# Pooling k of three batches on GpSimd and a DMA transpose in place of TensorE, in a pooled attention followed by a mixer

## The chip, the cores and the metric

The kernel runs on one core of a Trainium2 chip. The metric is device time in microseconds (us) of one execution. Three runs of the kernel before gave 282.7, 284.07 and 284.22 us, a median of 284.07. The profile comes from one further execution of 283.01 us, whose span (first to last recorded instruction) is 281.1 us. All places in time below are us from the start of that span.

## The reference

Inputs are `q`, `k`, `v` of shape (8 batches, 8 heads, 576 tokens, 64), and four weights. Everything is kept in float32 outside and bf16 inside the kernel.

```
k_p = k.reshape(B, H, 72, 8, 64).mean(axis=3)        # pool 8 neighbouring tokens
v_p = v.reshape(B, H, 72, 8, 64).mean(axis=3)
scores = scale * q @ k_p^T ;  attn = softmax(scores)  # 576 x 72 per head
x = (attn @ v_p) as (batch, 576 tokens, 512 channels)
u = x + (relu(x^T @ w_tok1) @ w_tok2)^T               # token mixing
out = u + relu(u @ w_ch1) @ w_ch2                     # channel mixing, 512 -> 1536 -> 512
```

So each batch needs its keys pooled from 576 to 72 tokens and laid out with the 64 head channels on partitions, before its first score can be computed.

## The kernel before

**Tiling.** The 576 tokens of a batch are 512 "main" tokens (4 tiles of 128) and 64 "tail" tokens. Tails of two batches share one 128-row tile: the groups are (0, 7), (1, 2), (3, 4), (5, 6). For the groups (3, 4) and (5, 6) one `TailUnit` computes the tail scores of both batches in one go, so `TailUnit.do_S` (L423, matmuls L431) of batches 5 and 6 needs the pooled keys of 5 **and** of 6.

**Pooling k (`pool_k`, L259 to L285).** k is loaded with 4 tokens on a partition (`km`, 128 partitions) and a tail tile `kt`. 32 matmuls (L271) with `km` as the stationary operand against a 0/1-over-8 matrix `pool_m`, and 8 more (L275) for the tail, leave the pooled and transposed keys in two PSUM banks. Four copies (L284, L285; two on ScalarE, two on VectorE) put them into `kbd`, a block form in which one matmul scores two heads. There are three `kbd` buffers.

**Pooling v (`sum_v`, L296).** For batches above 1, v is loaded with all 8 tokens of a pool on one of 72 partitions (`vs`, two buffers, L133), and GpSimd adds them up in 12 instructions (L302, L303, L304, four of each) into `vpx`.

**Order of the work.** Instructions are issued in an order written out by hand: every engine, and the SP queue that issues output writes and DMA transposes, executes its own instructions strictly in that order. The backbone is `c_stream(b)`, the channel mixing of batch b: 12 pieces `do_GT` (4 matmuls each, L776; called GT below) and 12 pieces of output (4 matmuls each, L791; three pieces make one 128-token block, after which VectorE adds u at L801 and SP writes it out at L829; called o0.0 to o3.2), plus a tail block for every second batch. `weave` (L29) mixes into it a side stream that prepares later batches:

- `value_stream(b+1)` (L731): on SP, the DMA transpose of q of b+2 (`qT_dma`, L550); on GpSimd, `load_gated` (L750) of b+3, which copies one element of a finished probability transpose (L752), then issues the loads, then runs `sum_v`; on TensorE the value products `do_AV`; then the token mixing (`mix_stream`, L580: `do_AT`, `do_u`, and a DMA transpose `do_uT` on SP), with `pool_k` of b+2 after the two `do_AT` (where b+2 opens a group or stands alone in one).
- `score_stream(b+2)` (L701): for the two units a and c of the batch, `do_S` for three banks of heads (matmuls L330, then VectorE max L333 and subtract L335), `do_E` (exponential on ScalarE, L343), `do_PT` (DMA transpose of the probabilities on SP, L350); `pool_k` of the group's second batch between the scores of c; last the tail's `do_S`, `do_E`, `do_PT`.

`weave` goes by written costs (KP 900 for a `pool_k`, SC 1060 for a bank of scores, AV 1150, 690 for a `do_u`, 1080 for a `do_AT`, 864 for a piece of the main stream): the side stream starts once `delay` cost units of the main stream are done and is spread evenly so that it ends `lead` units before the main stream does, 1728 units or two pieces here.

PSUM has six rotating 2 KB banks named `pa`, used by nearly all products. The part of the program that matters most below is `c_stream(3)`, which carries `value_stream(4)` and `score_stream(5)`; it runs from 128.45 to 158.00 us.

Of the kernel before, what the change touches and what calls it, by code (L numbers as in the profile page):

```python
# [10 lines left out]
AF = mybir.ActivationFunctionType  # L11
ALU = mybir.AluOpType
# [3 lines left out]
class Stream:  # L16
# [5 lines left out]
    def add(self, cost, fn):  # L22
        self.items.append((cost, fn))
# [25 lines left out]
def kernel(  # L49
# [17 lines left out]
    nc = tc.nc  # L67
    B, H, S, D = q.shape
    P = 128
# [3 lines left out]
    POOL = 8  # L73
    SP = S // POOL
# [31 lines left out]
    group_of = {b: g for g, members in enumerate(groups) for b in members}  # L106
    slot_of = {b: members.index(b) for members in groups for b in members}
    half = [slice(0, TAIL), slice(TAIL, P)]
    main_t, tail_t = {}, {}
    x_main, x_tail, u_main, uT_main, u_tail, uT_tail, ATs = {}, {}, {}, {}, {}, {}, {}  # L110

# [7 lines left out]
    def load(b, which=(0, 1, 2)):  # L119
        g = group_of[b]  # L120
        if b not in tail_t:
            tail_t[b] = [tail_pool.tile([P, H, D], BF16, name=n) for n in ("kt", "qt")]
            if b == 2:
                for t in tail_t[b]:
                    nc.gpsimd.memset(t[half[0]], 0.0)
            else:
                tail_t[groups[g][1]] = tail_t[b]
        main_t.setdefault(b, [None] * 3)
        for i in which:
            src = (k, q, v)[i]  # L130
            if i == 2 and b > 1:

                vs = v_pool.tile([P, H, POOL, D], BF16, name="vs")  # L133
                for r in (slice(0, SPM), slice(SPM, SP)):
                    nc.gpsimd.dma_start(out=vs[r].rearrange("p h t d -> p h (t d)"),
                                        in_=src[b].rearrange("h (p t) d -> p h (t d)", t=POOL)[r])
                main_t[b][i] = vs
                continue
            mt = (v_pool.tile([P, H, POOL, D], BF16, name="vs")[:, :, 0:NJ, :] if i == 2 else
                  kv_pool.tile([P, H, NJ, D], BF16, name=("km", "qm")[i]))  # L140
            main_t[b][i], tt = mt, tail_t[b][i]
            nc.gpsimd.dma_start(out=mt.rearrange("p h j d -> p h (j d)"),
                                in_=src[b, :, 0:MAIN, :].rearrange("h (p j) d -> p h (j d)", j=NJ))

            for bb in [b] if g < 2 else groups[g] if slot_of[b] == 0 else []:
                nc.gpsimd.dma_start(out=tt[half[slot_of[bb]]], in_=src[bb, :, MAIN:S, :].rearrange("h p d -> p h d"))
# [49 lines left out]
    NB = 3  # L196
    kbd = [singles.tile([P, H, 2, SP], BF16, name=f"kbd{i}") for i in range(NB)]
    vpx = [singles.tile([SP, H, D + 1], BF16, name=f"vpx{i}") for i in range(NB)]
    for i in range(NB):
        eng = nc.vector if i == 0 else nc.any  # L200
        eng.memset(kbd[i], 0.0)
        eng.memset(vpx[i][:, :, D], float(POOL))

    NPB = 4
    prob_m = [singles.tile([P, 2, H, P], BF16, name=f"prob_m{i}") for i in range(NPB)]
    prob_t = [singles.tile([P, 2, HP, P], BF16, name=f"prob_t{i}") for i in range(2)]
# [52 lines left out]
    def pool_k(b):  # L259
        pool_k_copy(b, pool_k_sum(b))  # L260

    def pool_k_sum(b):
        g, s = group_of[b], slot_of[b]
        km, kt = main_t[b][0], tail_t[b][0]
        kp_ps = [ps.tile([P, HP, SP], FP32, name="pa") for _ in range(2)]
        if b == 0:
            keep_running(kp_ps[0].rearrange("p r n -> p (r n)"), 22)
        for pr in range(HP):
            for j in range(NJ):
                for hl in range(2):  # L270
                    nc.tensor.matmul(out=kp_ps[hl][hl * D:(hl + 1) * D, pr, 0:SPM], lhsT=km[:, 2 * pr + hl, j, :],  # L271
                                     rhs=pool_m[:, 0:SPM], start=(j == 0), stop=(j == NJ - 1))
        for pr in range(HP):
            for hl in range(2):
                nc.tensor.matmul(out=kp_ps[hl][hl * D:(hl + 1) * D, pr, SPM:SP], lhsT=kt[:, 2 * pr + hl, :],  # L275
                                 rhs=pool_t[s][:, SPM:SP], start=True, stop=True)
        return kp_ps
# [17 lines left out]

    def sum_v(b):  # L296

        vs, add = main_t[b][2][0:SP], ALU.add
        for h0 in range(0, H, 2):
            hs = slice(h0, h0 + 2)  # L300
            s4 = sum_pool.tile([P, 2, 4, D], FP32, name="s4")[0:SP]
            nc.gpsimd.tensor_tensor(out=s4, in0=vs[:, hs, 0:4], in1=vs[:, hs, 4:8], op=add)  # L302
            nc.gpsimd.tensor_tensor(out=s4[:, :, 0:2], in0=s4[:, :, 0:2], in1=s4[:, :, 2:4], op=add)  # L303
            nc.gpsimd.tensor_tensor(out=vpx[b % NB][:, hs, 0:D], in0=s4[:, :, 0], in1=s4[:, :, 1], op=add)  # L304

    class Unit:

# [31 lines left out]
        def do_E(self, i):  # L339
            h0, h1 = BANKS[i]  # L340
            if self.probs is None:
                self.probs = prob_m[(2 * self.b + self.jj) % NPB]
            nc.scalar.activation(out=self.probs[:, :, h0:h1, 0:SP].rearrange("p e h n -> p h e n"),  # L343
                                 in_=self.sh[i][:, 0:(h1 - h0) * 2].rearrange("p (h e) n -> p h e n", e=2),
                                 func=AF.Exp, scale=scale)

        def do_PT(self, e):
            self.pT[e] = pt_pool.tile([P, H, P], BF16, name="pT")
# [54 lines left out]
    class TailUnit:  # L403
# [39 lines left out]
        def do_E(self):  # L443
            self.probs = prob_t[self.g % 2]
            for i, sh in enumerate(self.sh):
                nc.scalar.activation(out=self.probs[:, i, :, 0:SP], in_=sh[:, 0:HP], func=AF.Exp, scale=scale)

        def do_PT(self):
            n = len(self.bs) * HP
# [130 lines left out]
    def mix_stream(st, b, pooled=()):  # L580

        g, s = group_of[b], slot_of[b]
        add = adder(st)
        if b:
            u_main[b] = u_pool.tile([P, NJ, DM], BF16, name="um")
        uT_main[b] = u_pool.tile([P, 4, MAIN], BF16, name="uTm")
        if s == 1:
            u_tail[g] = ut_pool.tile([P, DM], BF16, name="ut")
            uT_tail[g] = ut_pool.tile([P, 4, P], BF16, name="uTt")
        do_AT, do_both_AT, do_u, do_uT, do_xT, do_uT0 = token_mix(b)  # L590
        if b == 0:
            return do_both_AT, do_xT, do_uT0
        add(1080, do_AT, 0)
        add(1080, do_AT, 1)
        for bb in pooled:
            add(KP, pool_k, bb)
        nj = NJ + s
        for j in range(nj + 1):
            if j < nj:
                add(690, do_u, j)  # L600
            if j >= 1:
                add(0, do_uT, j - 1)
# [93 lines left out]
    def owned(b):  # L696

        g, s = group_of[b], slot_of[b]
        return [b] if g < 2 else groups[g] if s == 0 else []

    def score_stream(st, b):  # L701

        add = adder(st)
        a, c, t = parts[b]
        own = owned(b)
        if b == 3:
            add(KP, pool_k, b)
        add(SC, a.do_S, 0)
        add(SC, a.do_S, 1)
        add(0, a.do_E, 0)  # L710
        add(SC, a.do_S, 2)
        add(0, a.do_E, 1)
        add(0, a.do_E, 2)
        add(0, a.do_PT, 0)
        add(0, a.do_PT, 1)
        add(SC, c.do_S, 0)
        for bb in own[1:]:
            add(KP, pool_k, bb)
        add(SC, c.do_S, 1)
        add(0, c.do_E, 0)  # L720
        add(SC, c.do_S, 2)
        add(0, c.do_E, 1)
        add(0, c.do_E, 2)
        add(0, c.do_PT, 0)
        add(0, c.do_PT, 1)
        if t:
            add(2 * SC, t.do_S)
            add(0, t.do_E)
            add(0, t.do_PT)

    def value_stream(st, b):  # L731

        add = adder(st)
        a, c, t = parts[b]
        if b + 1 < B:
            units(b + 1)
            add(0, qT_dma, b + 1)
        if b + 2 < B:
            add(0, load_gated, b + 2, lambda: t.pT[:, 0, 0:1] if t else c.pT[1][:, 0, 0:1])
        add(AV, a.do_AV, 0)  # L740
        add(AV, a.do_AV, 1)
        add(AV, c.do_AV, 0)
        add(AV, c.do_AV, 1)
        if t:
            add(AV, t.do_AV)
        mix_stream(st, b, owned(b + 1)[:1] if b + 1 < B and b != 2 else ())
# [3 lines left out]
    def load_gated(b, ready):  # L750

        nc.gpsimd.tensor_copy(out=gate, in_=ready())  # L752
        if b == 4:

            load(b - 1, (2,))
            load(b, (0, 2, 1))
            sum_v(b - 1)
        else:
            load(b, (0, 2, 1) if slot_of[b] else (0, 1, 2))
        sum_v(b)  # L760

    def channel_mix(uTs, us, dst, width, early=0):
# [91 lines left out]
    with tc.manual_schedule(engines=engines):  # L854
        weave(Stream(), first_stream())
        for b in range(B):
            side = Stream()
            if b == 0:
                second_stream(side)
            elif b + 1 < B:  # L860
                value_stream(side, b + 1)
            if b + 2 < B:
                score_stream(side, b + 2)

            weave(c_stream(b), side, (2592.0, 3456.0)[b] if b <= 1 else 1728.0, 3456.0 if b == B - 2 else 1728.0)


# [28 lines left out]
```

## Time and profile before

| what | value |
|---|---|
| median of three runs | 284.07 us (282.7 to 284.22) |
| profiled execution | 283.01 us, span 281.1 us |
| TensorE busy | 270.1 us, 96% of the span |
| VectorE, ScalarE, GpSimd busy | 57%, 44%, 37% |
| GpSimd's last sum | 184.63 to 185.1 us; nothing after |
| `c_stream(3)`, start to end | 128.45 to 158.00 us |
| one `sum_v` on GpSimd | 12 instructions, 10.17 us (145.32 to 155.49) |

How to read it: the page gives busy time by engine, the span in 40 slices, the chain of work that ended last, and groups of instructions by line. The timeline lists instructions as start, duration, engine, line, operation and tiles, with the idle time just before and who ended it. A matmul's duration includes its way through the array; matmuls in sequence start closer together than they last. "SPq" rows are instructions of the SP queue, whose duration is the time that issuing took; a transfer lands later.

### The profile page before, as it was taken

The numbers are of one execution on the slowest core, as the hardware profiler recorded it, in microseconds if no ns is written. First come the engines' busy times: TensorE is split into PE (matmuls) and PEld (weight loads), VectorE is DVE, ScalarE is ACT, GpSimd is POOL, SyncE is SP. The second block draws the span as 40 slices with busy tenths as digits, with TensorE's granted clock in tenths as the row PEclk, the third lists the DMA queues.
The fourth block names the chain that finished last, engine by engine and source line by source line (L and its number), as shares of the span: only waits on it lengthen the run. The fifth ranks groups of instructions, "written<-read, shape, count | busy, mean of one in ns | idle before, by whom it ended". The sixth has DMA issues, their size and how long they took to land.

```text
span 281.1 us, 5671 instructions
## 1 busy us (share of the span) xinstructions
PE 270.1 (96%) x2221; PEld 146.2 (52%) x2258; DVE 161.1 (57%) x368; ACT 122.6 (44%) x223; POOL 104.4 (37%) x153
## 2 busy tenths in 40 slices
PE   6799999999999999999999999999999999999995
PEld 4575565565445444475545454475444444554463
DVE  4695297597559952784469753775369542520012
ACT  8582896336515453045533552054514550037220
POOL 8666543590639958058429161830000000000000
PEclk9999999999999999999999999999999999999999
DMA  7999999999999999999996899659135901341013
GB/s 81 181 204 199 193 206 196 197 168 224 171 161 180 181 229 148 197 223 174 169 186 143 182 204 190 138 150 209 28 75 128 190 20 40 94 112 40 37 40 113
DMA packets 99963, 42.16 MB, mean 150 GB/s; under 512 B 69728, under 2 KB 95328, under 8 KB 99936
## 3 DMA queue, kind: packets, MB, share of 16 engines
q0 software_dynamic: 36016, 17.93, 49.2%
q1 hardware_dynamic: 63776, 23.74, 42.0%
q8 instruction: 18, 0.29, 0.4%
q10 hardware_dynamic: 144, 0.13, 0.1%
q14 instruction: 9, 0.07, 0.1%
HBM read 35.85 MB, written 9.44 MB: 161 GB/s over the span
## 4 chain that ended last, share of the span: by engine, by line
PE 84%; DMA 9%; POOL 4%; issue 1%; DVE 0%; ACT 0%; POOLq 0%
PE pa L791 33%; PE pa L776 30%; PE pa L513 4%; PE pa L479 4%; DMA qm<-in_q_dram 4%; DMA GT<-in_moe_w_tok_dram 3%; PE pa L394 3%; PE pa L330 3%; DMA pT<-prob_t 2%; PE pa L271 1%; PE pa L518 1%; PE pa L483 1%; PE pt L319 1%; POOL qm L152 1%; PE pt L357 1%
## 5 line engine op out<-in xcount | busy, mean ns | idle before, releaser
L791 PE MATMUL pa<-wc,GT 128*128 128x512 bf16 (+1 forms) x427 | 102.3, 373 | 0.9 <-issue 0.2
L778 ACT ACTIVATE GT<-pa 128x512 bf16<-128x512 f32 x105 | 62.3, 597 | 64.6 <-PE pa L776 59.5
L776 PE MATMUL pa<-uTm,wc 128*128 128x512 bf16 x356 | 88.6, 379 | 0.7
L776 PEld LDWEIGHTS <-wc 128*128 128x128 bf16 x564 | 44.9, 98 | 35.9 <-issue 0.3
L791 PEld LDWEIGHTS <-GT 128*128 128x128 bf16 x444 | 41.5, 98 | 40.7
L343 ACT ACTIVATE prob_m<-sh 128x432 bf16<-128x432 f32 (+1 forms) x48 | 24.5, 521 | 50.5 <-DVE sh L335 30.6
L302 POOL TENSOR_TENSOR s<-vs 72x512 f32<-72x512 bf16 x24 | 27.6, 1149 | 35.4 <-DMA vs<-in_v_dram 33.9
L801 DVE TENSOR_TENSOR o<-pa,um 128x512 f32<-128x512 f32 (+1 forms) x29 | 19.3, 669 | 25.3 <-PE pa L791 24.2
L335 DVE TENSOR_TENSOR sh<-pa,mx 128x432 f32<-128x432 f32 (+1 forms) x48 | 26.8, 558 | 5.1 <-ACT GT L778 0.5
L333 DVE TENSOR_REDUCE mx<-pa 128x6 f32<-128x432 f32 (+1 forms) x48 | 26.4, 550 | 3.4 <-PE pa L330 3.3
L399 DVE TENSOR_TENSOR xm<-pa,den 128x256 bf16<-128x256 f32 x56 | 23.8, 425 | 1.9
L398 DVE RECIPROCAL den<-pa 128x4 f32<-128x4 f32 (+1 forms) x66 | 11.7, 177 | 20.9 <-PE pa L394 20.7
L515 DVE TENSOR_TENSOR um<-pa,xm 128x512 bf16<-128x512 f32 x28 | 18.8, 688 | 8.1 <-PE pa L513 7.9
L475 DVE TENSOR_SCALAR AT<-pa 128x512 bf16<-128x512 f32 x8 | 5.5, 692 | 22.3 <-PE pa L483 20.8
L303 POOL TENSOR_TENSOR s<-s 72x256 f32<-72x256 f32 x24 | 17.4, 723 | 1.9
L394 PEld LDWEIGHTS <-pT 72*128 72x128 bf16 (+1 forms) x280 | 12.3, 100 | 9.7 <-issue 1.3
L330 PE MATMUL pa<-kbd,qT 128*128 128x144 bf16 x128 | 15.4, 226 | 0.5 <-ACT qT L321 0.5
L513 PE MATMUL pa<-AT,w2m 128*128 128x512 bf16 x56 | 15.8, 379 | 0.1
L330 PEld LDWEIGHTS <-qT 128*128 128x128 bf16 x128 | 10.6, 98 | 8.8 <-ACT qT L321 1.4
L394 PE MATMUL pa<-vpx,pT 72*128 72x65 bf16 (+1 forms) x280 | 14.1, 194 | 1.0 <-ACT pT L457 0.5
L479 PE MATMUL pa<-xm,w1m 128*128 128x512 bf16 x56 | 14.4, 379 | 0.1
L776 PE MATMUL pa<-uTt,wc 128*128 128x128 bf16 x192 | 11.9, 219 | 0.0
(126 smaller groups left out, 240.5 us busy)
## 6 DMA issues: line engine op xcount, KB each, us to landing
out_dram<-o SPq DMA_DIRECT2D x31, 256.0 KB, 2.8
km<-in_k_dram POOLq DMA_DIRECT2D x8, 512.0 KB, 8.5
vs<-in_v_dram POOLq DMA_DIRECT2D x8, 512.0 KB, 10.9
qm<-in_q_dram POOLq DMA_DIRECT2D x7, 512.0 KB, 12.2
wc<-in_moe_w_ch_dram POOLq DMA_DIRECT2D x6, 512.0 KB, 12.3
out_dram<-o SPq DMA_DIRECT2D x9, 128.0 KB, 2.5
kt<-in_k_dram POOLq DMA_DIRECT2D x8, 64.0 KB, 7.5
qm<-in_q_dram POOLq DMA_DIRECT2D x2, 256.0 KB, 5.1
```

The costliest lines, as they stand in the source:

```text
L302: nc.gpsimd.tensor_tensor(out=s4, in0=vs[:, hs, 0:4], in1=vs[:, hs, 4:8], op=add)
L330: nc.tensor.matmul(out=sc[:, (h - h0) * 2:(h - h0) * 2 + 2, :], lhsT=qTs[self.b][:, 2 * h + self.jj, :], rhs=kbd[self.b % NB][:, h], start ...
L333: nc.vector.tensor_reduce(out=mx[:, 0:n], in_=sc, axis=AX.X, op=ALU.max)
L335: nc.vector.tensor_tensor(out=sh[:, 0:n], in0=sc, in1=mx[:, 0:n, None].broadcast_to([P, n, SP]), op=ALU.subtract)
L343: nc.scalar.activation(out=self.probs[:, :, h0:h1, 0:SP].rearrange("p e h n -> p h e n"), in_=self.sh[i][:, 0:(h1 - h0) * 2].rearrange("p ...
L394: nc.tensor.matmul(out=ao[r, hh, :], lhsT=probs_of(h, r), rhs=vpx[b % NB][:, h, :], start=True, stop=True)
L399: nc.vector.tensor_tensor(out=xo[rows, hf * HP * D:(hf + 1) * HP * D].rearrange("p (h d) -> p h d", d=D), in0=ao[rows, :, 0:D], in1=den[ro ...
L479: nc.tensor.matmul(out=at_ps, lhsT=w1m[:, j, m * P:(m + 1) * P], rhs=x_main[b][:, j, :], start=(j == 0), stop=False)
L513: nc.tensor.matmul(out=u_ps, lhsT=w2m[:, m, j, :], rhs=ATs[b][:, m, :], start=(m == 0), stop=(m == 1))
L776: nc.tensor.matmul(out=g_ps[:, i, :], lhsT=wc1[:, kk, m * P:(m + 1) * P], rhs=uTs[:, kk, :], start=(kk == 0), stop=(kk == 3))
L778: nc.scalar.activation(out=GT[:, m0:m0 + per, :], in_=g_ps, func=AF.Relu)
L791: nc.tensor.matmul(out=hold["ps"], lhsT=GT[:, kk, j * P:(j + 1) * P], rhs=wc2[:, kk, cols], start=(kk == 0), stop=(kk == NM - 1 and us is ...
```

## The change

For batches 5, 6 and 7 (`KSUM`) k is loaded as v is: eight tokens of a pool on one of 72 partitions, in the same two-buffer pool `vs` (no tail tile of k is loaded). In `load_gated`, after the loads of such a batch, GpSimd first sums k with the 12 instructions of `sum_v` (now `sums_of`) into `ksum`, a tile that held batch 0's tail of k, and then sums v. `ksum_T` transposes `ksum` by one DMA transpose on SP (128x512, bf16) into `ksT`, and `ksum_copy` brings that into `kbd` with four VectorE copies. The sum is not divided by 8; the exponential's scale is divided by 8 in its place (`scale_of`). `pool_k` of these batches, 40 matmuls each and two ScalarE copies, is gone.

In the order: `ksum_T` of 5 and of 7 stands first in the side streams of `c_stream(3)` and `c_stream(5)`, ahead of `qT_dma`; `ksum_copy` of 5 and 7 stands where `pool_k` stood, with cost 0. Of batch 6, `ksum_T` stands after the last `do_S` of unit c of batch 5, `ksum_copy` after `c.do_PT(0)`; the tail's `do_S`, `do_E` and `do_PT` of (5, 6) leave the side stream and are put into the main stream ahead of its last two pieces.

```diff
+    KSUM = (5, 6, 7)
@@ load
-            if i == 2 and b > 1:
+            if i == 2 and b > 1 or i == 0 and b in KSUM:
...
+    ksum = tail_t[0][0]
+    ksT = tail_t[0][2].rearrange("p h d -> p (h d)").rearrange("p (r n) -> p r n", n=P)
...
+    def ksum_T(b):
+        nc.sync.dma_start_transpose(out=ksT, in_=ksum.rearrange("p h d -> p (h d)"))
+
+    def ksum_copy(b):
+        heads = kbd[b % NB].rearrange("p (r t) e n -> p r t e n", t=2)
+        for hl in range(2):
+            src = ksT[hl * D:(hl + 1) * D, :, 0:SP]
+            nc.vector.tensor_copy(out=heads[0:D, :, hl, 0, :], in_=src)
+            nc.vector.tensor_copy(out=heads[D:P, :, hl, 1, :], in_=src)
...
     def sum_v(b):
-        vs, add = main_t[b][2][0:SP], ALU.add
+        sums_of(main_t[b][2][0:SP], vpx[b % NB][:, :, 0:D])
+
+    def sums_of(vs, dst):
+        add = ALU.add
...
-            nc.gpsimd.tensor_tensor(out=vpx[b % NB][:, hs, 0:D], in0=s4[:, :, 0], in1=s4[:, :, 1], op=add)
+            nc.gpsimd.tensor_tensor(out=dst[:, hs], in0=s4[:, :, 0], in1=s4[:, :, 1], op=add)
+
+    def scale_of(b):
+        return scale / POOL if b in KSUM else scale
@@ mix_stream
         for bb in pooled:
-            add(KP, pool_k, bb)
+            if bb in KSUM:
+                add(0, ksum_copy, bb)
+            else:
+                add(KP, pool_k, bb)
@@ score_stream
+        late = [bb for bb in own[1:] if bb in KSUM]
         for bb in own[1:]:
-            add(KP, pool_k, bb)
+            if bb not in KSUM:
+                add(KP, pool_k, bb)
         add(SC, c.do_S, 1)
         add(0, c.do_E, 0)
         add(SC, c.do_S, 2)
+        for bb in late:
+            add(0, ksum_T, bb)
         add(0, c.do_E, 1)
         add(0, c.do_E, 2)
         add(0, c.do_PT, 0)
+        for bb in late:
+            add(0, ksum_copy, bb)
         add(0, c.do_PT, 1)
+        if t and late:
+            return [(0, t.do_S), (0, t.do_E), (0, t.do_PT)]
         if t:
             add(2 * SC, t.do_S)
...
@@ value_stream
             units(b + 1)
+            for bb in owned(b + 1)[:1]:
+                if bb in KSUM:
+                    add(0, ksum_T, bb)
             add(0, qT_dma, b + 1)
@@ load_gated
+        if b in KSUM:
+            sums_of(main_t[b][0][0:SP], ksum[0:SP])
         sum_v(b)
@@ the loop over batches
             if b + 2 < B:
-                score_stream(side, b + 2)
+                last = score_stream(side, b + 2)
+            at = len(main.items) - 2
+            main.items[at:at] = last
```

More of the change, by code (lines that the diff above doesn't have):

```diff
@@ L344, in do_E @@
                                  in_=self.sh[i][:, 0:(h1 - h0) * 2].rearrange("p (h e) n -> p h e n", e=2),
-                                 func=AF.Exp, scale=scale)
+                                 func=AF.Exp, scale=scale_of(self.b))
         def do_PT(self, e):
@@ L445, in do_E @@
             for i, sh in enumerate(self.sh):
-                nc.scalar.activation(out=self.probs[:, i, :, 0:SP], in_=sh[:, 0:HP], func=AF.Exp, scale=scale)
+                nc.scalar.activation(out=self.probs[:, i, :, 0:SP], in_=sh[:, 0:HP], func=AF.Exp,
+                                     scale=scale_of(self.bs[0]))
         def do_PT(self):
@@ L729, in score_stream @@
             add(0, t.do_PT)
+        return []
     def value_stream(st, b):
@@ L856 @@
         for b in range(B):
-            side = Stream()
+            side, main, last = Stream(), c_stream(b), []
             if b == 0:
@@ L862 @@
             if b + 2 < B:
-                score_stream(side, b + 2)
-            weave(c_stream(b), side, (2592.0, 3456.0)[b] if b <= 1 else 1728.0, 3456.0 if b == B - 2 else 1728.0)
+                last = score_stream(side, b + 2)
+            at = len(main.items) - 2
+            main.items[at:at] = last
+            weave(main, side, (2592.0, 3456.0)[b] if b <= 1 else 1728.0, 3456.0 if b == B - 2 else 1728.0)
 _INS = ['q', 'k', 'v', 'moe_w_tok1', 'moe_w_tok2', 'moe_w_ch1', 'moe_w_ch2']
```

## The prediction

> **What bounds the kernel now.** I read the page first: busy time, the slices, the shares of the chain of work that ended last.
>
> ```profile
> PE 270.1 (96%) x2221; PEld 146.2 (52%) x2258; DVE 161.1 (57%) x368; ACT 122.6 (44%) x223; POOL 104.4 (37%) x153
> PE   6799999999999999999999999999999999999995
> POOL 8666543590639958058429161830000000000000
> PE 84%; DMA 9%; POOL 4%; issue 1%; DVE 0%; ACT 0%; POOLq 0%
> ```
>
> TensorE (PE) is busy from the second slice to the end and is 84% of the chain: a us of TensorE work taken out is a us gained, a us in which TensorE waits is a us lost. GpSimd (POOL) has room, but not everywhere. Next the timeline around a `pool_k`, here batch 7's:
>
> ```profile
> 200.52 1.03 PE L776 MATMUL pa<-uTm,wc 128*128 128x512 bf16 x4
> 201.47 0.69 PE L271 MATMUL pa<-pool_m,km 128*64 128x64 bf16 x32
> 202.00 0.27 PE L275 MATMUL pa<-pool_t,kt 128*64 128x8 bf16 x8
> 202.20 1.04 PE L776 MATMUL pa<-uTm,wc 128*128 128x512 bf16 x3
> ```
>
> 40 short matmuls cost what stands between two groups: four matmuls at their pitch of 0.2155 take 0.86 us, so after 200.52 the next group could start at 201.38; it starts at 202.20: 0.82 us. Third, the timeline where batch 5's scores end in `c_stream(3)`:
>
> ```profile
> 153.19 0.29 PE L330 MATMUL pa<-kbd,qT 128*128 128x144 bf16 x2
> 153.40 0.69 DVE L801 TENSOR_TENSOR o<-pa,um 128x512 f32<-128x512 f32 x1
> 154.01 0.60 DVE L333 TENSOR_REDUCE mx<-pa 128x6 f32<-128x432 f32 x1
> 154.28 0.32 PE L431 MATMUL pa<-kbd,qTt 64*64 64x72 bf16 x16
> 155.23 0.45 DVE L333 TENSOR_REDUCE mx<-pa 128x4 f32<-128x288 f32 x1
> ```
>
> The tail scores (L431) follow the last bank of scores (L330) after one output piece. VectorE (DVE) handles that bank (155.23) 2 us after TensorE made it: it lags here. Last, GpSimd, and the SP queue's waits (total, times, longest):
>
> ```profile
> 131.95 0.46 POOL L304 TENSOR_TENSOR vpx<-s 72x128 bf16<-72x128 f32 x1
> 132.78 0.19 POOL L752 COPY gate<-pT 128x1 bf16<-128x1 bf16 x1 [0.37 <-DMA pT<-prob_m]
> 133.27 0.94 POOL L142 DMA_DIRECT2D km<-in_k_dram  x1 [0.30 <-issue]
> 145.32 1.14 POOL L302 TENSOR_TENSOR s<-vs 72x512 f32<-72x512 bf16 x1 [8.96 <-DMA vs<-in_v_dram]
> ```
> ```profile
> SPq L829 <- DVE o L801: 61.1, 15, 11.8
> ```
>
> GpSimd's sum of v of batch 5 ends just ahead of the gate for batch 6's loads. And SP stands still at each output write until VectorE has made the block: what is queued behind waits too.
>
> **The change, part by part.** *Removed:* three `pool_k`, 3 x 0.82 = 2.5 us of TensorE's path. The ScalarE copies go at no gain, ScalarE being idle over half the time; VectorE gets four copies in place of two.
>
> *Loads.* One km issue (0.92 us) and the kt issues (0.69 each) become two issues like vs (1.3 us a pair): GpSimd saves up to 1 us a batch; the bytes are equal.
>
> *Batch 5.* Its load is issued at 106.3. The nearest landings: km there 6.2 us, vs first in a row 9.4 to 9.8 (at 71.7, beside busy queues). GpSimd starts the sum of k at 112.5 to 116, ends 10.2 us later at 122.7 to 126.2, and the sum of v, whose data were there at 122, ends at 133 to 136.5, not at 132.4. So the gate for batch 6 comes 0.5 to 3.7 us late; I take 1.2, nearer to the km landing, since that is this very place. Batch 5's `ksum_T` (SP reaches it at 132.1) waits for nothing, its copy at 140 neither; `qT_dma` slips by one issue, 1.25 us, covered by the 9 us until its first score.
>
> *Batch 6.* k is issued at 134.5, lands 8.1 (km at 133.27) to 9.6 us later, and is summed by 152.8 to 154.3; with the late gate 157.5. Now the order. The side's cost falls from 20490 to 16570 (900 for each of two `pool_k`, 2 x 1060 for the tail) over the main stream's 24 x 864 - 3456 = 17280. `c.do_S(2)` comes when 15510/16570 = 0.94 is passed, that is after 21 pieces (0.95); after the 22nd (1.0) all that is left, cost 0, comes at once: `ksum_T(6)`, `c.do_E`, `c.do_PT(0)`, `ksum_copy(6)`, `c.do_PT(1)`, then the tail's `do_S`, then the last two pieces. One piece, 0.86 us, is all that TensorE has between that bank and the tail scores, and in that time the keys of 6 must be transposed and copied.
>
> TensorE, walked through this order with its own durations (12 GT and 10 output pieces of 0.862; AV 0.26; AT 1.08; u 0.43, the fifth 0.86; a bank 0.19 or 0.13) from 128.45, arrives at the tail's `do_S` at 154.2. VectorE, from the fifth u at 146.5, runs one add of u (0.69), two of output, three banks of unit a and three of c (1.28 each, the third 0.97): its output block 2 is done at 155.7, and the last bank at 156.7. SP queues the write of block 2 (0.4) ahead of `ksum_T(6)`, so that issues at 156.25, whenever GpSimd was done before. It lands 2.5 us (a lone 128x512 transpose, tail of q) to 3.7 us (median of those of u) later; I take 3.0, as for the tail's probabilities: 159.2. Four copies of 64x288 take at most 0.46 each (L284, from PSUM in f32) and, at the rate of the bf16 copy L359 (72x1024 in 0.677 against 0.425 for 512 at L321, so 0.5 ns per element and 0.17 fixed), 0.31: 1.4 us with gaps. `kbd` is ready at 160.7, TensorE stands from 154.2 to 160.8: **6.6 us** lost (bounds 5.3, lone transpose and copies of 0.2; 9, landing 4.4, copies of 0.46 and GpSimd 1 us later than SP). Nothing covers this: the two pieces and the next stream are queued behind on TensorE. `c.do_PT` and the tail's probabilities slip behind `ksum_T(6)` on SP by some 1.3 and 6 us, but `c_stream(4)` begins late by as much, and needs the tail's only 9.8 us into it. The gate of batch 7's loads slips from 163.6 to 166.4; its sums end by 196, its `ksum_T` stands in `c_stream(5)` (from 195), its copy at 206: no wait.
>
> *The clock.* At the start the matmuls are slow (timeline, then the same line in two stretches, ns as least/median/most):
>
> ```profile
> 2.19 5.46 PE L257 MATMUL pa<-idle 128*128 128x288 bf16 x22 [2.19 <-DVE pool_t L182]
> L257 PE MATMUL pa<-idle x6: 447/447/448, 2.6 to 3.8; 128*128 128x288 bf16 x6
> L257 PE MATMUL pa<-idle x8: 286/346/379, 8.7 to 12.6; 128*128 128x432 bf16 x4, 128*128 128x512 bf16 x2, 128*128 128x288 bf16 x2
> ```
>
> 128x288 takes 447 ns there and 286 later; 22 take 5.46 us where the later pitch (288/512 x 0.2155 = 0.121) gives 2.7. So TensorE coming out of rest loses 2.8 us before it runs at full rate, though the granted clock reads 1.00. Whether 6.6 us of standing puts it back, no row shows: 0.94 us (the longest wait, at 13.9) did not; the rest before the start, of at least 2.19 us, had it slow. 6.6 is nearer to that side; I take 2.7, bounds 0 and 3.4 (a slower start than this one's by a quarter). By the Trainium skill, "TensorE: Matmul & The Clock Gate", Part 1, a whole idle window of about 3.4 us halves the clock and about 3.4 us of sustained work frees it; by that the term would be an estimated 1.7 to 3.4 us and all but sure.
>
> Sum: 283.0 - 2.5 + 6.6 + 2.7 = **289.8 us**. This goes by the profiled execution, 283.01 us, which lies 0.4% below the median of 284.07 and inside the three runs' spread.
>
> **Rivals.** (1) *The stall without the slow restart*: 283.0 - 2.5 + 6.6 = 287.1. For it: no row shows a slow stretch after the start; against it: none of the waits there is near 6 us. (2) *The copies collide with GpSimd.* From 154 to 164 GpSimd sums v of 6 without a gap (0.08 us between instructions); if each VectorE copy, bf16 from SBUF, has to let the running sum instruction finish, it loses up to 1.15 us, some 0.55 on average: 289.8 + 4 x 0.55 = 292.0. The trace speaks neither way, since no VectorE copy of bf16 between SBUF tiles lies beside a sum. The Trainium skill, "SBUF — State Buffer", Who interferes with whom, says that the two engines share a port pair under an exclusive lock; by that this case would happen. (3) *GpSimd is the one that is late*: k of 5 and of 6 landing after 10 us each put the end of the sum at 158, 1.7 us past SP: 291.5. (4) **The other side: the transpose is hidden.** If `kbd` of 6 is ready when TensorE gets there, only the PSUM bank freed by block 2's add (155.7) holds it, 1.5 us: 283.0 - 2.5 + 1.5 = 282.0, faster. It decides at `ksum_T(6)` issuing by 155.7 - 4.4 = 151.3; for it speaks that a landing of 6.2 us as in batch 5 would end the sum at about 151; against it, SP's place behind the write at 155.7. It needs the order to differ from the one worked out.
>
> **How the numbers follow.** Forecast 0.50; rival 1 0.18; rival 2 0.13; rival 3 0.09; rival 4 0.06; another stall or none, 0.04. The forecast's own bounds are 288 to 292.5, rival 1's 285.8 to 288. The range 285.8 to 293 takes in the first two and most of 2 and 3, leaving out rival 4 and the far ends. About 0.5%, 1.4 us, is what a measurement of this kernel can tell: faster 0.06 (rival 4), same 0.04, slower 0.90.
>
> **What would show it.** After: no L271 or L275 behind 100 us; 36 instead of 24 instructions of each sum line on GpSimd; a wait of TensorE ahead of L431 near 154 us, 5 to 9 us, released by `ksum_copy` on VectorE, that one by the DMA of `ksT`; its SP issue right behind a write at L829; `c_stream(4)` starting near 162.5. Slow matmuls for some 5 us behind the wait confirm the clock term, copies of over 0.5 us rival 2, an SP wait on GpSimd rival 3. The prediction is wrong if L431 follows without a wait, or if TensorE has other work there.

## The result, and the profile after

The changed kernel takes 294.95 us (median of four runs, 292.19 to 298.37) against 284.14: 1.0376 times the kernel before, 95% interval 1.0315 to 1.0437. It is slower, as forecast, but by 10.7 us where 5.7 to 6.8 were forecast, and it lies outside the range. The profiled execution took 295.01 us, with a span of 293.3 us against 281.1. One note on reading the comparisons below: they leave out runs more than 1.5% above the fastest of the same kernel; where a kernel's own waits come and go from run to run (pooling k of batch 6 on TensorE), I therefore give the median of all its runs.

The page of the changed kernel: busy time, slices, shares of the chain.

```profile
PE 274.0 (93%) x2138; PEld 145.2 (50%) x2138; DVE 161.5 (55%) x374; ACT 120.6 (41%) x217; POOL 131.1 (45%) x189
PE   7899999999999699999939499999999999999994
POOL 8666634752359985997299434994000000000000
PEclk9999999999999999999997989999999999999999
PE 70%; DMA 15%; POOL 10%; DVE 2%; issue 1%; ACT 0%; POOLq 0%; DVEq 0%
```

TensorE's row was all nines from the third slice to the last but one; now it has holes in slices 14, 21 and 23, and behind the last two (22 and 24) the granted clock falls, which it never did before. TensorE's share of the chain went from 84% to 70%, DMA's and GpSimd's from 13% to 25%. The chain is followed back by inference, and its GpSimd part is too large: it runs through the sum of v of batch 6, for which the tail's scores do not wait (the sum of k of 6 had ended at 155.0). The timeline of TensorE in `c_stream(3)`:

```profile
148.46 1.03 PE L831 MATMUL pa<-wc,GT 128*128 128x512 bf16 x4
154.02 0.38 PE L352 MATMUL pa<-kbd,qT 128*128 128x144 bf16 x3 [4.53 <-DMA qT<-qm]
154.22 1.89 PE L831 MATMUL pa<-wc,GT 128*128 128x512 bf16 x4
...
162.84 0.22 PE L453 MATMUL pa<-kbd,qTt 64*64 64x72 bf16 x1
166.41 0.22 PE L453 MATMUL pa<-kbd,qTt 64*64 64x72 bf16 x2 [3.35 <-DVE kbd L274]
167.16 0.29 PE L453 MATMUL pa<-kbd,qTt 64*64 64x72 bf16 x13 [0.53 <-DVE kbd L275]
167.39 3.15 PE L831 MATMUL pa<-wc,GT 128*128 128x512 bf16 x8
```

There are two waits, not one. The second is the predicted one: the tail scores (L453, L431 before) wait for `ksum_copy` (L274, L275). The first was not predicted: batch 5's first scores (L352) stand 4.53 us for the transpose of q. Behind the first, a group of four matmuls takes 1.89 us and not 1.03; behind the second, eight take 3.15 and not 1.89. The stretches of two us (busy time, then the granted clock third from the end) say why:

```profile
153.00:155.00 2.00, 0.98 (x5) 0.47 (x6) 0.57 (x1) 0.00 (x0) 1.84 (x3) 0.81 1.11 104
155.00:157.00 2.00, 2.00 (x8) 0.95 (x7) 1.15 (x3) 0.56 (x1) 1.81 (x3) 0.50 1.40 124
157.00:159.00 2.00, 2.00 (x10) 0.91 (x9) 1.48 (x4) 0.56 (x1) 1.77 (x4) 0.84 1.44 91
...
167.00:169.00 2.00, 1.84 (x18) 0.79 (x18) 1.41 (x5) 0.44 (x1) 0.00 (x0) 0.72 0.97 178
169.00:171.00 2.00, 2.00 (x6) 0.76 (x5) 0.86 (x2) 0.44 (x1) 0.00 (x0) 0.50 0.04 12
171.00:173.00 2.00, 2.00 (x16) 1.00 (x15) 0.40 (x2) 0.86 (x2) 0.00 (x0) 0.93 0.85 163
```

What is missing to a clock of 1.00 adds up to 0.38 + 1.00 + 0.32 = 1.70 us behind the first wait and 0.56 + 1.00 + 0.14 = 1.70 behind the second: 3.4 us at half rate each time.

And the queues behind the first wait, SP's issues and GpSimd's gate and load, in one order of time (`vt<-kt` is `ksum_T`: `ksT` and `ksum` are tiles that held a tail of v and of k and go by the old names):

```profile
134.30 1.25 SPq L268 DMA_TRANSPOSE vt<-kt  x1
135.09 0.19 POOL L790 COPY gate<-pT 128x1 bf16<-128x1 bf16 x1 [1.07 <-DMA pT<-prob_m]
135.35 1.29 POOL L137 DMA_DIRECT2D vs<-in_k_dram  x2
135.64 6.23 SPq L576 DMA_TRANSPOSE qT<-qm  x1
```

`ksum_T` (L268) takes the place that `qT_dma` (L576) had, and `qT_dma` issues 0.3 us behind the first load of batch 6 where it had been 1.1 us ahead of it (132.17 against 133.27). Its issue alone then takes 6.23 us, not 1.74, and it lands 18.3 us after issue, not 3.8. The two transposes by their lines, before and after:

```profile
L553 SPq DMA_TRANSPOSE qT<-qm x1: 1742/1742/1742, 132.2 to 132.2; - x1
DMA to landing us min/median/max: 3.8/3.8/3.8
```
```profile
L576 SPq DMA_TRANSPOSE qT<-qm x1: 6227/6227/6227, 135.6 to 135.6; - x1
DMA to landing us min/median/max: 18.3/18.3/18.3
```

Where the 12.2 us of span went, by the places where the parts of the program begin (before, after):

| part | before | after | difference |
|---|---|---|---|
| up to the start of `c_stream(3)` | 128.45 | 130.57 | +2.1 |
| `c_stream(3)` | 29.55 | 39.77 | +10.2 |
| `c_stream(4)` (starts 158.00, 170.34) | 32.40 | 32.88 | +0.5 |
| `c_stream(5)` (starts 190.40, 203.22) | 28.71 | 27.87 | -0.8 |
| from there to the end | 62.0 | 62.2 | +0.2 |

Inside `c_stream(3)`: wait for q 4.5, wait of the tail 4.3 (162.84 to 167.39, less the 0.25 that the scores take), half rate 1.7 and 1.2 (the other 0.5 falls into the next stream), two `pool_k` less, 1.65. That is 10.05. The 2.1 us ahead of it are two waits, 1.66 us for a transpose of u and 0.93 for one of probabilities, at 95 to 100 us (the hole in slice 14), ahead of the first instruction that the change touches. The same pair of waits stands in the profiles of e7 and e9 below (1.3 and 1.0, 1.7 and 0.8) and is missing or under 1 us in the others, with the same instructions there; so I take them for a matter of the execution, not of the change. They look like the same thing at another place: the transposes of u issued at 79.6 to 87.7, beside the loads of 71.8 to 97.1, landed after 9.7 to 14.2 us here, after 8.7 to 10.8 in the profile before. They are not what brings the first wait: e3's profile below has none of them and has q's wait.

### The profile page after: what moved, and what is told of

Read it like the earlier page. It is cut to its first block, busy times and chain, and to the rows that moved or that the text cites. A ratio compares the mean times of both kernels' runs of the same rounds, so it can differ in the third digit from the quotient of the medians.

```text
span 293.3 us, 5509 instructions
## 1 busy us (share of the span) xinstructions
PE 274.0 (93%) x2138; PEld 145.2 (50%) x2138; DVE 161.5 (55%) x374; ACT 120.6 (41%) x217; POOL 131.1 (45%) x189
## 4 chain that ended last, share of the span: by engine, by line
PE 70%; DMA 15%; POOL 10%; DVE 2%; issue 1%; ACT 0%; POOLq 0%; DVEq 0%
PE pa L816 27%; PE pa L831 27%; DMA pT<-prob_m 4%; PE pa L536 4%; PE pa L502 4%; DMA qm<-in_q_dram 4%; DMA GT<-in_moe_w_tok_dram 3%; POOL s L320 3%; DMA vs<-in_k_dram 3%; PE pa L416 3%; POOL s L321 2%; PE pa L352 2%; PE pa L541 1%; PE pa L506 1%; DMA vt<-kt 1%
## 5 line engine op out<-in xcount | busy, mean ns | idle before, releaser
L831 PE MATMUL pa<-wc,GT 128*128 128x512 bf16 (+1 forms) x444 | 106.8, 381 | 0.0
L816 PE MATMUL pa<-uTm,wc 128*128 128x512 bf16 x372 | 89.8, 380 | 1.7 <-DMA uTm<-um 1.7
L831 PEld LDWEIGHTS <-GT 128*128 128x128 bf16 x444 | 42.1, 99 | 42.2 <-issue 2.2
L320 POOL TENSOR_TENSOR s<-vs 72x512 f32<-72x512 bf16 x36 | 41.3, 1148 | 26.0 <-DMA vs<-in_k_dram 13.6
L321 POOL TENSOR_TENSOR s<-s 72x256 f32<-72x256 f32 x36 | 26.0, 721 | 2.8
L352 PE MATMUL pa<-kbd,qT 128*128 128x144 bf16 x128 | 15.7, 229 | 5.0 <-DMA qT<-qm 4.5
L352 PEld LDWEIGHTS <-qT 128*128 128x128 bf16 x128 | 10.7, 99 | 14.1 <-DMA qT<-qm 5.0
L262 PE MATMUL pa<-idle 128*128 128x288 bf16 (+2 forms) x36 | 10.1, 411 | 2.2 <-DVE pool_t L184 2.2
## 6 DMA issues: line engine op xcount, KB each, us to landing
qm<-in_q_dram POOLq DMA_DIRECT2D x7, 512.0 KB, 14.2
```

Of the source, the lines that this page charges most:

```text
L352: nc.tensor.matmul(out=sc[:, (h - h0) * 2:(h - h0) * 2 + 2, :], lhsT=qTs[self.b][:, 2 * h + self.jj, :], rhs=kbd[self.b % NB][:, h], start ...
L816: nc.tensor.matmul(out=g_ps[:, i, :], lhsT=wc1[:, kk, m * P:(m + 1) * P], rhs=uTs[:, kk, :], start=(kk == 0), stop=(kk == 3))
L831: nc.tensor.matmul(out=hold["ps"], lhsT=GT[:, kk, j * P:(j + 1) * P], rhs=wc2[:, kk, cols], start=(kk == 0), stop=(kk == NM - 1 and us is ...
```

## The experiments

Theory A: the transpose of q is late because it runs beside batch 6's loads, into which `ksum_T` has pushed it. Theory B: it is the new form of k's loads, eight tokens on a partition, that slows transposes. The comparisons are with runs of the kernel before on the same chip (medians 282.5 to 282.9 us).

**q's transpose ahead again (e1).**

```diff
+            add(0, qT_dma, b + 1)
             for bb in owned(b + 1)[:1]:
                 if bb in KSUM:
                     add(0, ksum_T, bb)
-            add(0, qT_dma, b + 1)
```

> The changed kernel with one thing other: on SP, qT_dma of batches 5 and 7 stands ahead of ksum_T, not behind it. Theory A (order): ksum_T ahead of it pushed qT_dma of 5 by 1.3 us, past the point where the loads of batch 6 begin to move, and a transpose that runs beside these loads takes 18 us to land and not 4. Here qT_dma is ahead again: it lands in 4 to 6 us, TensorE's wait of 4.5 us ahead of batch 5's first scores and the half-rate stretch behind it (1.7 us) are gone; ksum_T of 5 is now the one beside the loads and lands late, 10 us or more, which is partly covered (its copy is due 6 us later): 0 to 6 us come back. Total: 0 to 6 us under the changed kernel, 1.016 to 1.038 of the kernel before. Theory B (form): loads of k with eight tokens on a partition slow every transpose beside them, wherever it stands: qT still takes over 10 us, time as the changed kernel, 1.038.

Measured: 295.24 us, 1.0415 (1.0359 to 1.047), no better than the changed kernel. One of its four runs, the profiled one, took 470.62 us at a granted clock of 0.559, so the waits are read from one more run of the same kernel.

> The kernel of e1_qt_first once more, for its profile, since that of the first time lies in an execution with TensorE slowed throughout. It took 295 us: theory A has qT in time here and ksum_T(5), now beside the loads, landing 10 us late or more; VectorE then stands at ksum_copy(5), and TensorE behind it for want of PSUM banks, 4 to 8 us. Theory B: qT lands 15 us or more after issue and TensorE waits at batch 5's scores as in the changed kernel.

Measured: 295.05 us. q lands 6.6 us after issue and nobody waits for it. TensorE's waits, and VectorE's timeline:

```profile
PE pa L541 <- DVE um L538: 5.0, 1, 5.0
PE pa L453 <- DVE kbd L274: 3.7, 1, 3.7
```
```profile
146.50 0.23 DVE L274 COPY kbd<-vt 64x288 bf16<-64x288 bf16 x1 [6.88 <-DMA vt<-kt]
146.74 0.39 DVE L275 COPY kbd<-vt 64x288 bf16<-64x288 bf16 x1
147.14 1.21 DVE L274 COPY kbd<-vt 64x288 bf16<-64x288 bf16 x1
148.37 0.79 DVE L275 COPY kbd<-vt 64x288 bf16<-64x288 bf16 x1
149.18 1.29 DVE L538 TENSOR_TENSOR um<-pa,xm 128x512 bf16<-128x512 f32 x2
```

The transpose that now stands last, `ksum_T(5)`, lands 11.8 us after issue in place of 2.5. VectorE stands 6.88 us at its copy, and with the adds of u queued behind it TensorE runs out of PSUM banks and stands 5.0 us. Whoever comes second pays, which is theory A; the cover of 6 us, which I had counted on in part, is far too small. The time alone could not have told A from B.

**The kernel before with one spare transpose (e2) and with three (e6)** ahead of `qT_dma` of batch 5:

```diff
+    def spare_T():
+        nc.sync.dma_start_transpose(out=<the tile that ksT uses>, in_=<kt0>)
...
+            if b == 4:
+                add(0, spare_T)        # e6: three times
             add(0, qT_dma, b + 1)
```

> The kernel before, with one DMA transpose more on SP, 128x512, just ahead of qT_dma of batch 5; nothing reads what it writes, and all pooling stays on TensorE. Theory A (order): it alone is enough: qT_dma of 5 issues behind the first load of batch 6, lands 10 to 18 us later, TensorE waits 2 to 5 us ahead of batch 5's first scores (L330) and runs at half rate behind it: 1.012 to 1.025 of the kernel before. Theory B (form): the loads are those of before, so qT lands in 4 to 6 us and the time is that of before, 1.000.

Measured: 282.87 us, 0.9997 (0.9959 to 1.0034). The time is theory B's, the landing is A's: q lands 11.7 us after issue with the loads of before, at 145.67, and TensorE comes to the first scores at 146.75. So the time could not tell.

> The kernel before with three spare transposes ahead of qT_dma of batch 5 in place of one (nothing reads what they write). With one, qT landed 11.7 us after issue in place of 3.8, just in time. Theory A: three put its issue some 2.7 us behind the first load of batch 6; it lands 15 to 20 us after issue, TensorE waits 4 to 8 us ahead of batch 5's first scores and runs at half rate for 3.4 us behind that: 1.015 to 1.035 of the kernel before, with every load and every pooling as before. Theory B (only loads of the new form do such harm): qT lands within 13 us, no or a short wait: 1.000 to 1.010.

Measured: 287.99 us, 1.017 (1.0138 to 1.0202), with every load and every pooling as before. Not quite as expected in its mechanism: SP's issues and TensorE's wait are

```profile
131.37 13.99 SPq L260 DMA_TRANSPOSE vt<-kt  x3
145.45 1.68 SPq L556 DMA_TRANSPOSE qT<-qm  x1
```
```profile
149.23 0.54 PE L333 MATMUL pa<-kbd,qT 128*128 128x144 bf16 x3 [3.55 <-DMA qT<-qm]
```

The first spare lands after 2.4 us; the second, issued at 133.8 beside the loads, after 10.3; the third writes the same tile and waits for it on SP until 144.2. q, behind them, issues at 145.45 and lands in 3.7 us. TensorE stands 3.55 us, and the clock reads 0.50 for 3.4 us around and behind that. A transpose beside the old loads is slow too, and what it holds up on SP reaches TensorE. Theory B, that only the new form does this, falls. That the new form makes it somewhat worse is possible: q landed after 18.3 and 21.2 us beside loads of k in the new form, after 11.7 and 15.5 beside the old; the places differ too, so this stays open.

**k of 6 back on TensorE (e4).** `KSUM = (5, 7)`; the tail goes back to the side stream, `ksum_T(5)` stays ahead of `qT_dma`.

```diff
-    KSUM = (5, 6, 7)
+    KSUM = (5, 7)
@@ ksum_copy: the sums are divided by 8 here, not in the exponential
-            nc.vector.tensor_copy(out=heads[...], in_=src)
+            nc.vector.tensor_scalar(out=heads[...], in0=src, scalar1=1.0 / POOL, scalar2=None, op0=ALU.mult)
```

> The changed kernel, but k of batch 6 is pooled by TensorE as before, so that the tail's do_S, do_E and do_PT go back to the end of the side stream and ksum_T(6), ksum_copy(6) are gone; k of 5 and 7 stay on GpSimd, their sums divided by 8 in the copy on VectorE (the exponential's scale is the old one). ksum_T(5) stays ahead of qT_dma. Theory: the tail's wait (4.3 us) and the half rate behind it (1.7) go, one pool_k (0.8) comes back; qT's wait (4.5 and 1.7) stays: 5.2 us under the changed kernel, 1.016 to 1.022 of the kernel before. If the two waits have one cause in batch 6's load in the new form (theory B), both go, and the time is 0.994 of the kernel before.

Measured: ten runs from 281.29 to 287.83 us, median 286.9, 1.014 of 282.88 (the three fastest alone, 281.29 to 284.83, give 1.0013, 0.9956 to 1.007). In its profile the tail's wait is gone and q's is there (k of 6 is loaded in the old form here):

```profile
PE pa L358 <- DMA qT<-qm: 3.4, 1, 3.4
```

q lands 15.5 us after issue, and behind the wait the clock reads 0.50 for 6.8 us. The fastest run, 281.29, may be what is left when q comes in time; only one run, of 287.54 us, was profiled, so this is not shown.

**Filling the tail's wait (e3).**

```diff
-            return [(0, t.do_S), (0, t.do_E), (0, t.do_PT)]
+            return [(0, lambda: warm(18)), (0, t.do_S), (0, t.do_E), (0, t.do_PT)]
```

> The changed kernel with 18 matmuls of zeros (128x512, 3.9 us at full rate) ahead of the tail's do_S of batches 5 and 6, where TensorE stood for 3.9 us; they are extra work and change no result. If the half rate behind that wait (granted clock 0.50 for 3.4 us, 1.7 us lost) comes from TensorE's having stood still, it is gone here, and the time is 1.2 to 1.7 us under the changed kernel, about 1.033 of the kernel before. If it has another cause (power, the transfers), the clock falls all the same and the time is that of the changed kernel or up to 1 us above.

Measured: 292.28 us, 1.0321 (1.0241 to 1.0402), that is 0.0055 or some 1.6 us less than the changed kernel's 1.0376, within intervals that overlap. The profile is clearer: the filler, and stretches with the clock third from the end.

```profile
162.89 4.05 PE L262 MATMUL pa<-idle 128*128 128x512 bf16 x18
```
```profile
165.00:167.00 2.00, 2.00 (x12) 0.80 (x11) 0.54 (x3) 0.00 (x0) 0.00 (x0) 1.00 0.69 136
167.00:169.00 2.00, 1.64 (x23) 0.80 (x20) 1.50 (x5) 0.17 (x1) 0.00 (x0) 1.00 1.03 190
169.00:171.00 2.00, 2.00 (x11) 0.94 (x10) 1.22 (x3) 1.18 (x3) 0.00 (x0) 1.00 0.07 14
```

The keys are as late as before, but TensorE worked meanwhile, and the clock stays at 1.00 where it was 0.72 and 0.50. The half rate comes from standing still. (Behind q's wait, which was 7.4 us here and unfilled, it fell to 0.50 too, and for 6.8 us. With this longer first wait the time of e3 is no measure of what the filler gains; the clock in the rows is.)

**The first wait alone taken away (e9).** Batch 6's loads wait for both transposes of q; `ksum_T(5)` behind them; the tail as in the changed kernel.

```diff
-            add(0, load_gated, b + 2, lambda: t.pT[:, 0, 0:1] if t else c.pT[1][:, 0, 0:1])
+            add(0, load_gated, b + 2, lambda: parts[5][2].qT[:, 0, 0:1] if b == 4 else
+                t.pT[:, 0, 0:1] if t else c.pT[1][:, 0, 0:1])
```

> The changed kernel with only the first wait taken away: ksum_T(5) behind qT_dma, and the loads of batch 6 gated by the transposed tail of q of batch 5. The tail's wait stays, so this is what the prediction priced: TensorE at the tail's do_S about 154, keys of 6 in kbd about 160.7, or up to 1 us later, since the gate now holds the loads. Theory: a wait of 5 to 8 us there and 1.7 us of half rate, less 2.5 us: 1.014 to 1.028 of the kernel before. Rival: the tail's wait in the changed kernel was itself a child of the first (the late transposes), and is gone with it: 0.992 to 1.002.

Measured: 290.93 us, 1.0258 (1.0203 to 1.0313). q lands in 3.8 us. In it q's transpose is as prompt as the prediction took it to be, and its tail's wait is the predicted one (TensorE's timeline, then VectorE's):

```profile
156.69 0.22 PE L453 MATMUL pa<-kbd,qTt 64*64 64x72 bf16 x1
161.44 0.27 PE L453 MATMUL pa<-kbd,qTt 64*64 64x72 bf16 x2 [4.53 <-DVE kbd L274]
163.99 0.40 PE L453 MATMUL pa<-kbd,qTt 64*64 64x72 bf16 x13 [2.29 <-DVE kbd L275]
```
```profile
160.98 0.40 DVE L274 COPY kbd<-vt 64x288 bf16<-64x288 bf16 x1 [2.58 <-DMA vt<-kt]
161.41 1.20 DVE L275 COPY kbd<-vt 64x288 bf16<-64x288 bf16 x1
162.62 0.78 DVE L274 COPY kbd<-vt 64x288 bf16<-64x288 bf16 x1
163.42 0.52 DVE L275 COPY kbd<-vt 64x288 bf16<-64x288 bf16 x1
```

From 156.69 to 164.32, less 0.25, TensorE loses 7.4 us. `ksum_T(6)` issues at 158.26, right behind an output write on SP (157.64); the copies take 2.9 us together where 0.93 would do, because GpSimd is summing v of 6:

```profile
161.38 1.15 POOL L320 TENSOR_TENSOR s<-vs 72x512 f32<-72x512 bf16 x1
162.60 0.72 POOL L321 TENSOR_TENSOR s<-s 72x256 f32<-72x256 f32 x1
163.40 0.45 POOL L322 TENSOR_TENSOR vpx<-s 72x128 bf16<-72x128 f32 x1
```

The second, third and fourth copy overlap these three adds: the second ends at 162.61 where the add of 161.38 ends at 162.52, the third at 163.40 and the fourth at 163.94, each under 0.1 us behind an add. The clock reads 0.50 for 6.8 us here, of which TensorE works 4.2: some 2.1 us lost.

**Two batches, both waits gone (e5), and its control (e10).** `KSUM = (5, 7)` as in e4, with e9's gate and order.

> k of 5 and 7 on GpSimd, k of 6 on TensorE as in the run before; ksum_T behind qT_dma on SP; and the loads of batch 6 gated by one element of the transposed tail of q of batch 5 (the second transpose of qT_dma), so that none of them moves before both transposes of q have landed. Theory A (transposes beside loads): qT lands in about 4 us, no wait of TensorE at batch 5's scores, no half rate; the loads begin 4 us later, which batch 6's keys, due 14 us later, can bear. Two pool_k are saved: 2 x 0.8 = 1.6 us, 0.994 of the kernel before (0.990 to 0.998), and the spread of the run before (281 to 288 us) goes. If the waits had another cause than the loads, the time stays at 1.010 to 1.018.

Measured: 281.23 us, 0.995 (0.9928 to 0.9973), twelve runs from 280.92 to 283.24. It beats both kernels. SP and GpSimd now run in this order, q landing in 3.9 us:

```profile
131.62 1.79 SPq L582 DMA_TRANSPOSE qT<-qm  x1
133.51 1.24 SPq L441 DMA_TRANSPOSE qTt<-qt  x1
136.02 0.19 POOL L797 COPY gate<-qTt 128x1 bf16<-128x1 bf16 x1 [3.65 <-DMA qTt<-qt]
136.25 0.93 POOL L149 DMA_DIRECT2D km<-in_k_dram  x1
```

> The kernel before with one line other: the loads of batch 6 are gated by the transposed tail of q of batch 5, as in e5_gate_on_qT; all pooling of k stays on TensorE. It tells whose gain the 0.995 of e5_gate_on_qT is. If it is that of the two pool_k taken out (1.6 us), the time here is that of before, 0.998 to 1.002; if the gate itself helps (fewer transposes beside loads), it is 0.994 to 0.997.

Measured: 282.74 us, 1.0026 (0.9991 to 1.006). The gate alone gains nothing, so the gain of e5, 1.5 us, comes with the pooling; it is of the size of the two `pool_k`.

**All three batches, the tail later (e7, e8).** Gate and order of e9; the tail's scores of (5, 6) and `ksum_copy(6)` moved into `c_stream(4)`.

```diff
@@ score_stream: the tail's three steps go; ksum_T(6) behind c.do_PT (e7), ahead of c.do_E (e8)
@@ value_stream(5)
         add(AV, a.do_AV, 1)
+        add(0, ksum_copy, 6)                 # e8: one value product later
         add(AV, c.do_AV, 0)
         add(AV, c.do_AV, 1)
+        add(0, t.do_S)                       # e8: cost 900
+        add(0, t.do_E)
+        add(0, t.do_PT)
+        add(4600, load_gated, 7, lambda: t.pT[:, 0, 0:1])   # e8: 3700
         add(AV, t.do_AV)
```

> All three batches on GpSimd, with both waits taken away: the loads of batch 6 gated as in e5_gate_on_qT and ksum_T behind qT_dma; ksum_T(6) behind both do_PT of unit c of batch 5; ksum_copy(6) and the tail's do_S, do_E, do_PT of (5, 6) moved into c_stream(4), behind its second and fourth value product; the tail's value product some five pieces later. If the two waits and what followed them are the whole loss, three pool_k come out: 283 - 2.5 = 280.5 to 281.5, 0.991 to 0.995 of the kernel before. If a wait stays: keys of 6 still late (GpSimd ends their sum at about 157) costs 0 to 2 us: up to 1.000.

Measured: 283.97 us, 1.0043 (1.0012 to 1.0074). VectorE reaches the copy 2.04 us ahead of `ksum_T(6)`'s landing, and TensorE stands behind it for a bank:

```profile
167.49 1.04 PE L822 MATMUL pa<-uTm,wc 128*128 128x512 bf16 x4 [2.12 <-DVE xm L421]
```

Behind this wait, too, the clock reads 0.50 for 3.4 us (168.44 to 171.85), so it costs some 3.8 us in the profiled run.

> e7_tail_later with the wait that its trace shows taken away (VectorE stood 2 us at ksum_copy(6), and TensorE behind it for a PSUM bank, since ksum_T(6) was queued behind two do_PT and landed at 165.3): ksum_T(6) goes ahead of c.do_E and c.do_PT of batch 5 again, ksum_copy(6) one value product later, the tail's do_S one piece later. If that was all, three pool_k come out: 0.991 to 0.995 of the kernel before; if a new wait comes in its place (the copies beside GpSimd's sum of v take up to 1.2 us each in place of 0.23), 0.996 to 1.004.

Measured: 281.91 us, 0.9975 (0.9953 to 0.9997). `c_stream(3)` shrinks to 27.5 us (128.23 to 155.75), 2.0 less than before, but `c_stream(4)` grows to 34.3 (to 190.05), 1.9 more: 0.26 are the tail's scores, which moved there, the tail's value product waits 0.7 us for its late transpose, and the rest are shorter gaps, not traced one by one. In this order the third batch gains nothing over e5.

## Why the prediction was right or wrong

Right: the sign; that `pool_k` is worth 0.8 us each (e5 takes out two, 1.6 us, and is 1.5 faster); the order around the tail's `do_S` and the wait there, with its releaser; SP's place behind the output write; the slow restart of TensorE.

Wrong, the step that failed: **"`qT_dma` slips by one issue, 1.25 us, covered by the 9 us until its first score."** The slip was right. What I left out is what it slips into: it fell behind the first load of batch 6. The cover of 9 us was held against a landing of 4, and the landing was 18.3. By the prediction's own gate, 1.2 us late, the load (134.5) would have stayed behind q's transpose (133.4); measured from the start of `c_stream(3)` the gate came 0.2 us late, and the two changed places. The prediction did not watch this order at all. The trace of before had a warning: the transposes of u issued at 79.6 to 86.7, beside loads that moved from 72 to 93, landed after 8.7 to 10.8 us, those at 142 to 148 after 2.4 to 5.6, and I used the median of them all, 3.7. But even 10.8 would have fitted into the nearly 13.9 us between q's issue (135.64) and TensorE's arrival at the scores (149.49), so the 18.3 could not be read there. This one step cost 4.5 us and a half-rate stretch of 1.7. Taken away (e9), the time is 1.0258 times that before, or 7.3 us above it, against the forecast sum of 6.8 above the profiled execution. That the two are so close is in part luck: in e9 the tail's wait is 0.8 us longer than forecast and the half rate costs 0.6 less.

Mis-sized: the tail's wait, 6.6 us forecast, is 4.3 in the changed kernel, since VectorE, SP and GpSimd went on during the first wait: `ksum_T(6)` issues 0.8 us behind TensorE's arrival and not 2.05, it lands after 2.5 us and not 3.0, and the copies take 1.0 and not 1.4. With the first wait gone it is 7.4 (e9), inside the bounds of 5.3 to 9. There `ksum_T(6)` issues 1.6 us behind TensorE's arrival and lands after 2.7, both sooner than forecast, and the excess over 6.6 is rival 2, the copies beside GpSimd's sum: 2.9 us in place of the 1.4 that I took, and e1's second run shows it at its worst, 1.21 us for a copy that takes 0.23 alone. The Trainium skill's rule ("SBUF — State Buffer", Who interferes with whom), an exclusive lock on a port pair that the two engines share, agrees with these rows. In the changed kernel itself the collision did not happen: GpSimd was done at 165.3, the copies began at 166.13 and took 0.23 each.

The clock term, 2.7 forecast, is 1.70 us at each of two waits in the changed kernel. Its size differs from run to run: the half rate lasted 3.4 us in the changed kernel, e6 and e7 and 6.8 in e1's second run, e3, e4 and e9 (in e9 it cost 2.1). The rule of the Trainium skill ("TensorE: Matmul & The Clock Gate", Part 1), a whole idle window of about 3.4 us to halve the clock and about 3.4 us of sustained work to free it, agrees with the two waits of the changed kernel; e7, where a wait of 2.12 us was enough, does not agree with it, and there the measurement holds. e3 shows the cause. Rival 1 (no slow restart) falls, rival 4 (transpose hidden) too; rival 3, GpSimd late for `ksum_T(6)`, did not occur: its sum of k of 6 ended at 155.0, `ksum_T(6)` issued at 163.64 behind the write of 163.22 (in e9 at 156.2 and 158.26).

The order of sizes, then: -2.5 + 4.3 + 1.7 as priced in kind, + 4.5 + 1.7 for the step that failed, + 2.1 of the profiled execution's own, is 11.8 of the 12.2 us.

## What to carry to other kernels

When a step is put ahead of others on a queue that issues transposes, look not at how long it delays them but at what they then run beside: here 1.3 us moved a transpose of 3.8 us into a block of loads, and it took 18. Where one depends on such an order, make it explicit, with the loads gated on the landed transpose; to check the cover against the slowest landing in the trace and not the median is better, but here would not have been enough (10.8 us against 18.3). And a kernel bound by TensorE pays for a longer wait twice, once standing and once at half rate: in these runs every wait of 2.1 us or more behind the start did so, and none of up to 1.7 us.

## What the runs showed of the hardware

- A DMA transpose of q or of the keys' sum that SP issued behind the first of batch 6's loads landed after 7.6 (the tail of q, kernel before) to 21.2 us (e3); one issued 0.8 us ahead of it (e1's second run) after 6.6, one issued 1.1 us ahead (kernel before) after 3.8; with none of these loads in flight, after 2.4 to 3.9. Its issue on SP can stretch too, from 1.7 to 5.5 (e4), 6.2 and 8.0 us (e3), though only to 1.9 in e2, and all that is queued behind it waits. The loads suffer as well: in the changed kernel v of batch 6 landed 17.7 us after issue, q of 6 after 21.4, where 10.5 and 12.2 were seen before. That both kinds share the same DMA engines whoever issues them is what the Trainium skill states ("DMA: Bandwidth & Descriptors", Issuing engines are not separate DMA queues), and these rows agree with it.
- TensorE's granted clock went to 0.50 at each wait of 2.12 us or more behind the start, and at none of up to 1.69. It fell between 2.6 us after TensorE had stopped (e4, still standing) and 1.5 us after it had resumed (changed kernel, 166.41 and 167.88), and it stayed at 0.50 for 3.4 or 6.8 us, never for a time between.
- VectorE's copy of 64x288 bf16 between SBUF tiles takes 0.23 us alone. The twelve such copies that took longer, 0.36 to 1.21 us (e1's second run, e7, e8, e9), ran beside GpSimd's adds, and each ended within 0.1 us behind the end of an add.
